# Packing two layers' attention rows from 0 to 79, and giving the weighted scores a third buffer

## The chip, the cores and the metric

One core of a Trainium2 chip runs the whole program. The metric is the device time of one execution in microseconds.

TensorE (PE in the views) multiplies: its stationary operand is loaded first (PEld), then the moving one follows. VectorE (DVE) and ScalarE (ACT) do the work between. The granted clock (PEclk) is the share of TensorE's full clock that the profile recorded; 1.00 is all of it. "Drain" stands here for the time lost when TensorE goes from one size of operand tile to another.

## The reference

Four layers over 2048 rows of 512: a memory-augmented recurrent attention layer (A), a gated feed-forward layer (B), and both again with the same weights.

```python
def _A_ref(x, mem0, Wq, Wk, Wv, Wo, seg_len):      # seg_len 32, 8 memory rows, 32 heads of 128
    ...
    for s in range(n_seg):                          # 64 segments, one after the other
        h = concat([mem, xs])                       # 8 + 32 = 40 rows
        q, k, v = h Wq, h Wk, h Wv
        p = softmax(where(mask, q k^T * scale, -1e9))
        o = (p v) Wo
        mem = o[:8]                                 # the next segment needs it
        outs.append(o[8:])
    ...
x = x + A(layernorm(x)); x = x + B(layernorm(x))
x = x + A(layernorm(x)); x = x + B(layernorm(x))
```

## The kernel before

A step handles segment t of the first attention layer and segment t-6 of the second at once, so there are 70 steps: 6 with layer 0 alone, 58 with both, 6 with layer 1 alone. In each step the 32 heads go through in six groups (five of 6, one of 2). A small planner in the kernel simulates the engines, takes each task with its duration, the buffers it needs and what it depends on, and fixes the order of instructions on every engine. So a change of the buffers or of the task list changes the order everywhere.

The score rows of layer 0 lie in partitions 0 to 39, those of layer 1 in 64 to 103; all stationary operands of scores and transposes are 128x128, padded.

```python
self.qku = [c.tile([P, 3, 2, P], BF16, ...) for i in range(3)]
self.pb  = [c.tile([P, HG, P], BF16, ...) for i in range(2)]        # weighted scores
... # (cut)
plo, phi = (0, LW) if both else ((0, JOFF) if j0 == 0 else (JOFF, LW))   # JOFF 64, LW 104
qc = [(JOFF, 2), (1, L)] if both else [(1, L)]                            # L 40
... # scores
nc.tensor.matmul(s_all(SB)[:, uh - h0 + i, :], lhsT=qku[:, i, 0, :], rhs=fview(qku[:, i, 1, q0:q0 + 1], qc), ...)
... # softmax on VectorE and ScalarE: mask, max, subtract, exp, sum, reciprocal (cut)
# rz: the reciprocal times 1 or 0, by layer
pl.add("DVE", 80, ... out=rz[...], in0=rs[...], in1=self.jm[...], op=ALU.mult ...)
# pb: exp times rz
pl.add("DVE", dve_ns(nj * n), pmul, r=[..., ("rz", gi)], w=[("pb", gi)])
# transposes
nc.tensor.matmul(o_ap, lhsT=pb[:, hl, :], rhs=idn, start=True, stop=True)
```

## Time and profile before

| | before |
|---|---|
| median of the runs beside the changed kernel | 1910.07 us |
| TensorE busy | 94% |
| VectorE busy | 67% |
| start to step 1 (weights arrive) | 106.6 us |
| steps 1 to 5, layer 0 alone | 104.2 us |
| steps 6 to 63, both layers | 1543.5 us |
| step 64 to the end, layer 1 alone and a last feed-forward block | 157.9 us |

The shares and stages are those of one profiled execution (span 1912.2 us). The stages are cut where each step's 128x32 matmuls of line 674 start for the first time; they stand once in every step. I take TensorE as the bound: it is busy for 97% of the two-layer stage, so that a microsecond of its time there should be nearly a microsecond of the whole; in the one-layer stages it has some idle time. The prediction below shows the lines.

### The profile page before, as it was taken

The page shows a single profiled execution, that of the slowest core. Times are in us where ns is not written, and L with a number is a line of the kernel's source. Part 1 is how long each engine was busy: PE and PEld are TensorE (multiplying, and loading weights), DVE is VectorE, ACT ScalarE, POOL GpSimd, SP SyncE. Part 2 cuts the span into 40 slices and gives each one's busy share as a digit, 9 for nine tenths or more (in the row PEclk, how much of TensorE's full clock was granted, in tenths as well). Part 3 has the DMA queues.
Part 4 walks back from the last instruction along what each step waited for, and adds up shares of the span by engine and source line. Part 5 has one row for each costly group of instructions (what it writes and reads, how often), then busy time and mean ns, then how long its engine had stood idle before and what let it go on. Part 6 is the DMA issues. An engine that isn't in the chain of part 4 may idle for free.

```text
span 1912.2 us, 94130 instructions
## 1 busy us (share of the span) xinstructions
PE 1804.7 (94%) x40891; PEld 1565.7 (82%) x41116; DVE 1287.3 (67%) x4238; ACT 1196.6 (63%) x2743; POOL 587.3 (31%) x840
## 2 busy tenths in 40 slices
PE   7988999999999999989999999999999999999986
PEld 3577788988888898878888898889888888988785
DVE  5366576777677666767777777767667666776663
ACT  5655566666666666656666666666666666665553
POOL 6512112332424142332414142332424142323222
PEclk9999999999999999999999999999999999999998
DMA  9723324554636364544635364554646364545543
GB/s 350 252 81 94 97 65 135 150 155 116 187 106 176 108 167 128 144 144 123 180 105 171 108 172 130 144 151 129 180 111 184 81 171 135 145 133 151 146 112 111
DMA packets 130129, 273.83 MB, mean 143 GB/s; under 512 B 29562, under 2 KB 61058, under 8 KB 129714
## 3 DMA queue, kind: packets, MB, share of 16 engines
q0 software_dynamic: 60608, 185.48, 33.8%
q1 hardware_dynamic: 69106, 82.32, 15.2%
q8 instruction: 322, 5.28, 1.2%
q14 instruction: 93, 0.76, 0.1%
HBM read 222.04 MB, written 27.26 MB: 130 GB/s over the span
## 4 chain that ended last, share of the span: by engine, by line
PE 83%; DVE 7%; DMA 3%; ACT 3%; issue 3%; POOL 0%; SPq 0%; DVEq 0%; ACTq 0%; POOLq 0%
PE bank L703 30%; PE bank L802 14%; PE bank L866 10%; PE bank L565 8%; PE bank L674 6%; PE bank L722 4%; PE bank L772 3%; PE bank L785 3%; PE bank L885 3%; DMA vsb<-sst 2%; DVE st L732 1%; ACT otsb L949 1%; PE bank L535 1%; DVE mx L737 1%; DVE pb L758 1%
## 5 line engine op out<-in xcount | busy, mean ns | idle before, releaser
L703 PE MATMUL bank<-hT,wq_sb 128*128 128x80 bf16 (+1 forms) x8960 | 626.1, 198 | 11.1 <-DVE hT L815 5.3
L703 PE MATMUL bank<-hT,wk_sb 128*128 128x80 bf16 (+1 forms) x8960 | 626.2, 199 | 2.9 <-issue 2.9
L949 ACT CAST qku<-bank 128x480 bf16<-128x480 f32 (+3 forms) x770 | 394.6, 513 | 253.1 <-PE bank L703 232.1
L703 PEld LDWEIGHTS <-wq_sb 128*128 128x128 bf16 x8960 | 460.3, 99 | 37.0 <-issue 16.5
L703 PEld LDWEIGHTS <-wk_sb 128*128 128x128 bf16 x8960 | 453.0, 100 | 3.3 <-issue 3.3
L732 DVE TENSOR_TENSOR st<-bank,maskb 64x240 f32<-64x240 f32 (+5 forms) x768 | 284.5, 371 | 223.9 <-PE bank L722 215.8
L802 PE MATMUL bank<-otsb,wo_sb 128*128 128x80 bf16 (+1 forms) x8960 | 372.0, 198 | 12.1 <-ACT otsb L949 9.6
L802 PEld LDWEIGHTS <-wo_sb 128*128 128x128 bf16 x8960 | 340.1, 99 | 24.4 <-issue 15.3
L858 POOL DMA_DIRECT2D wg<-in_B_w_gate_dram x224 | 169.6, 757 | 414.5 <-PE bank L866 382.0
L949 ACT CAST otsb<-bank 128x480 bf16<-128x480 f32 (+3 forms) x420 | 198.9, 486 | 88.8 <-PE bank L785 72.0
L880 POOL DMA_DIRECT2D wd<-in_B_w_down_dram x224 | 159.2, 712 | 280.8 <-PE bank L772 81.7
L523 POOL TENSOR_TENSOR lns<-lns,negh 128x1 f32<-128x1 f32 x78 | 44.2, 568 | 586.6 <-DVE lns L522 281.9
L758 DVE TENSOR_TENSOR pb<-st,rz 104x480 bf16<-104x480 f32 x348 | 206.7, 595 | 7.8 <-PE bank L772 2.7
L744 DVE TENSOR_REDUCE sm<-st 104x6 f32<-104x240 f32 (+5 forms) x420 | 154.0, 367 | 80.0 <-ACT st L742 78.2
L949 ACT CAST ptsb<-bank 128x480 bf16<-128x480 f32 (+3 forms) x343 | 168.6, 496 | 50.0 <-PE bank L772 45.8
L742 ACT ACTIVATE st<-st 104x240 f32<-104x240 f32 (+5 forms) x420 | 161.2, 384 | 57.4 <-DVE st L739 54.9
L866 PE MATMUL bank<-xnT,wg 128*128 128x128 bf16 x1792 | 175.4, 221 | 2.1 <-ACT xnT L949 1.4
L866 PE MATMUL bank<-xnT,wu 128*128 128x128 bf16 x1792 | 174.9, 221 | 2.0 <-DMA wu<-in_B_w_up_dram 2.0
L722 PE MATMUL bank<-qku 128*128 128x80 bf16 (+1 forms) x2240 | 169.3, 198 | 3.7 <-ACT qku L949 1.0
L859 POOL DMA_DIRECT2D wu<-in_B_w_up_dram x224 | 167.7, 749 | 3.0 <-PE bank L866 1.1
L873 DVE SCALAR_TENSOR_TENSOR hff<-th,bank 128x256 bf16<-128x256 f32 x224 | 92.3, 417 | 107.0 <-ACT th L871 104.7
L739 DVE TENSOR_TENSOR st<-st,mx 104x240 f32<-104x240 f32 (+5 forms) x420 | 157.4, 375 | 4.5
(91 smaller groups left out, 2499.3 us busy)
## 6 DMA issues: line engine op xcount, KB each, us to landing
wg<-in_B_w_gate_dram POOLq DMA_DIRECT2D x224, 256.0 KB, 4.4
wu<-in_B_w_up_dram POOLq DMA_DIRECT2D x224, 256.0 KB, 4.8
wd<-in_B_w_down_dram POOLq DMA_DIRECT2D x224, 256.0 KB, 4.8
vsb<-scr SPq DMA_DIRECT2D x512, 48.0 KB
vsb<-sst SPq DMA_DIRECT2D x280, 64.0 KB
scr<-vst SPq DMA_DIRECT2D x128, 96.0 KB
wv_sb<-in_A_Wv_dram SPq DMA_DIRECT2D x4, 1024.0 KB
wq_sb<-in_A_Wq_dram SPq DMA_DIRECT2D x5, 768.0 KB
```

Of the source, the lines that this page charges most:

```text
L703: nc.tensor.matmul(o_ap, lhsT=W[:, c, h * P:(h + 1) * P], rhs=mv(c), start=(c == 0), stop=(c == DC - 1))
L722: nc.tensor.matmul(s_all(SB)[:, uh - h0 + i, :], lhsT=qku[:, i, 0, :], rhs=fview(qku[:, i, 1, q0:q0 + 1], qc), start=True, stop=True)
L732: pl.add("DVE", dve_ns(n, True), lambda gsz=gsz, hs=hs, st=st, SB=SB, pj_=pj_, npj_=npj_, idx=idx: nc.vector.tensor_tensor(out=st[pj_, hs] ...
L739: pl.add("DVE", dve_ns(n), lambda gsz=gsz, hs=hs, st=st, mx=mx: nc.vector.tensor_tensor(out=st[pr, hs], in0=st[pr, hs], in1=mx[pr, hs].uns ...
L742: pl.add("ACT", act_ns(n), lambda hs=hs, st=st: nc.scalar.activation(out=st[pr, hs], in_=st[pr, hs], func=ACTF.Exp, scale=self.scale), r=s ...
L758: nc.vector.tensor_tensor(out=o, in0=st[pr, hs].unsqueeze(1).to_broadcast([npart, 2, gsz, L]), in1=rz[pr, :, 0:gsz].unsqueeze(3).to_broadc ...
L802: nc.tensor.matmul(WB[:, c * ncol:(c + 1) * ncol], lhsT=self.wo[:, h, c * P:(c + 1) * P], rhs=otsb[:, hl, 0:ncol], start=(h == 0 and c == ...
L858: pl.add("POOL", 760, lambda wg=wg, fs=fs: nc.gpsimd.dma_start(out=wg[:], in_=self.wgv[:, :, fs]), r=[("wo", self.H - 1)], w=[("wg", gi)] ...
L859: pl.add("POOL", 760, lambda wu=wu, fs=fs: nc.gpsimd.dma_start(out=wu[:], in_=self.wuv[:, :, fs]), r=[("wo", self.H - 1)], w=[("wu", gi)] ...
L866: nc.tensor.matmul(gu[:, 2 * i + k, :], lhsT=W[:, c, i * P:(i + 1) * P], rhs=xnT[:, c, :], start=(c == 0), stop=(c == DC - 1))
L880: pl.add("POOL", 760, lambda wd=wd, ip=ip: nc.gpsimd.dma_start(out=wd[:], in_=self.wdv[:, 2 * ip:2 * ip + 2, :]), w=[("wd", di)] + (["boot ...
L949: nc.scalar.copy(out=dst, in_=src)
```

## The change

The intent is a denser layout: with both layers in rows 0 to 79 the padded rows and columns go, the copies write contiguous columns, and the room saved in qku pays for a third buffer of weighted scores (pb). In one-layer steps the rows are always 0 to 39 and the product rz, which only separated the layers, goes. A path for transposing by DMA comes with it, but is switched off (DMAT = 0). Cut to its core:

```diff
-LW = JOFF + L                       # 104
+LW = 2 * L                          # 80
-self.qku = [c.tile([P, 3, 2, P], BF16, name=f"qku{i}") for i in range(3)]
+self.qku = [c.tile([P, 3, 2, LW], BF16, name=f"qku{i}") for i in range(3)]
-self.pb = [c.tile([P, HG, P], BF16, name=f"pb{i}") for i in range(2)]
+self.pb = [c.tile([LW, HG, P], BF16, name=f"pb{i}") for i in range(3)]
 ...
+pr = slice(0, ncol)                 # ncol: 80 for both layers, 40 for one
-nc.tensor.matmul(s_all(SB)[:, ...], lhsT=qku[:, i, 0, :], rhs=fview(qku[:, i, 1, q0:q0 + 1], qc), ...)
+nc.tensor.matmul(s_all(SB)[pr, ...], lhsT=qku[:, i, 0, 0:ncol], rhs=qku[:, i, 1, 0:ncol], ...)
 ...
-pl.add("DVE", 80, ... rz ...)
+if both: pl.add("DVE", 80, ... rz ...)
+elif t == self.NSEG and g < 3: pl.add("DVE", 300, ... memset of pb's old columns ...)
 ...
-nc.tensor.matmul(o_ap, lhsT=pb[:, hl, :], rhs=idn, start=True, stop=True)
+nc.tensor.matmul(pt_all(PB)[:, hl, :], lhsT=pb[pr, hl, :], rhs=self.ident[pr, pr], start=True, stop=True)
```

More of the change, by code (lines that the diff above doesn't have):

```diff
@@ L20 @@
 L = MEM + SEG
-JOFF = 64
-LW = JOFF + L
+LW = 2 * L
 KOFF = 8
 XS = 24
+SPT = 1000
+LATT = 2500.0
 SCOL = 24
@@ L368, in __init__ @@
         self.HG = 6
+        self.DMAT = 0
         self.x_in = x_in.rearrange("b s d -> (b s) d")
@@ L397, in setup_tiles @@
         self.maskb = c.tile([P, L], F32, name="maskb")
+        self.mask1 = c.tile([L, L], F32, name="mask1")
         self.jm = c.tile([P, 2], F32, name="jm")
@@ L444, in setup_consts @@
         nc.gpsimd.memset(self.maskb[:], 0.0)
-        tmpm = self.st[0][:, 0, :]
-        nc.gpsimd.memset(tmpm[0:L, :], 0.0)
-        nc.gpsimd.affine_select(out=tmpm[0:L, :], in_=tmpm[0:L, :], pattern=[[-1, L]],
+        nc.gpsimd.memset(self.mask1[:], 0.0)
+        nc.gpsimd.affine_select(out=self.mask1[:], in_=self.mask1[:], pattern=[[-1, L]],
                                 compare_op=ALU.is_ge, fill=NEG, base=0, channel_multiplier=1)
-        nc.gpsimd.memset(tmpm[0:MEM, :], 0.0)
-        nc.sync.dma_start(out=self.maskb[JOFF:LW, :], in_=tmpm[0:L, :])
+        nc.gpsimd.memset(self.mask1[0:MEM, :], 0.0)
+        nc.sync.dma_start(out=self.maskb[L:LW, :], in_=self.mask1[:])
         nc.gpsimd.affine_select(out=self.maskb[0:L, 0:SEG], in_=self.maskb[0:L, 0:SEG], pattern=[[-1, SEG]],
@@ L454, in setup_consts @@
         nc.vector.memset(self.jm[:], 0.0)
-        nc.vector.memset(self.jm[0:JOFF, 0:1], 1.0)
-        nc.vector.memset(self.jm[JOFF:P, 1:2], 1.0)
+        nc.vector.memset(self.jm[0:LW, 1:2], 1.0)
+        nc.vector.memset(self.jm[0:L, 0:1], 1.0)
+        nc.vector.memset(self.jm[0:L, 1:2], 0.0)
         for t_ in self.hT:
@@ L638, in emit_step @@
         ncol = 2 * L if both else L
-        plo, phi = (0, LW) if both else ((0, JOFF) if j0 == 0 else (JOFF, LW))
-        pr = slice(plo, phi)
-        npart = phi - plo
+        pr = slice(0, ncol)
+        npart = ncol
+        nt = -(-ncol // 16) * 16
         hkeys = [("hT", slot, j, k) for j in jobs for k in ("m", "x")]
@@ L653, in pt_all @@
             return B[:, 0:6 * ncol].rearrange("p (h k) -> p h k", h=6)
-        qc = [(JOFF, 2), (1, L)] if both else [(1, L)]
-        q0 = 0 if both else JOFF * j0
         for j in jobs:
@@ L659, in emit_step @@
             b, i = s // BLK, s % BLK
-            row = KOFF if j == 0 else JOFF
+            row = KOFF if j == 0 else KOFF + L + MEM + SEG - XS
             for k in range(4):
@@ L709, in qkcopy @@
                 def qkcopy(nh=nh, pq=pq, qku=qku):
-                    dst = fview(qku[:, 0, 0, q0:q0 + 1], [(P, 2 * nh)] + qc)
-                    src = pq[:, 0:2 * nh * ncol]
-                    if both:
-                        src = src.rearrange("p (m a b) -> p m a b", a=2, b=L)
-                    else:
-                        src = src.rearrange("p (m b) -> p m b", b=L)
-                    return dst, src
+                    return (fview(qku[:, 0, 0, 0:1], [(LW, 2 * nh), (1, ncol)]),
+                            pq[:, 0:2 * nh * ncol].rearrange("p (m b) -> p m b", b=ncol))
                 pl.add("ACT", act_ns(2 * nh * ncol, True), qkcopy, r=[pq], w=[qku])
@@ L721, in sc @@
                     for i in range(nh):
-                        nc.tensor.matmul(s_all(SB)[:, uh - h0 + i, :], lhsT=qku[:, i, 0, :], rhs=fview(qku[:, i, 1, q0:q0 + 1], qc),
+                        nc.tensor.matmul(s_all(SB)[pr, uh - h0 + i, :], lhsT=qku[:, i, 0, 0:ncol], rhs=qku[:, i, 1, 0:ncol],
                                          start=True, stop=True)
@@ L726, in emit_step @@
             gi = self.nxt("st", 2)
-            st, pb, mx, sm, rs = self.st[gi], self.pb[gi], self.mx[gi], self.sm[gi], self.rs[gi]
+            st, mx, sm, rs = self.st[gi], self.mx[gi], self.sm[gi], self.rs[gi]
+            bi = self.nxt("pb", 3)
+            pb = self.pb[bi]
             n = gsz * L
             for idx, j in reversed(list(enumerate(jobs))):
-                pj_ = slice(JOFF if not both and j else 0, JOFF if j == 0 else LW)
-                npj_ = pj_.stop - pj_.start
-                pl.add("DVE", dve_ns(n, True), lambda gsz=gsz, hs=hs, st=st, SB=SB, pj_=pj_, npj_=npj_, idx=idx: nc.vector.tensor_tensor(
+                pj_ = slice(0, L * (idx + 1))
+                npj_ = pj_.stop
+                mk = self.mask1 if j and not both else self.maskb
+                pl.add("DVE", dve_ns(n, True), lambda gsz=gsz, hs=hs, st=st, SB=SB, pj_=pj_, npj_=npj_, mk=mk, idx=idx: nc.vector.tensor_tensor(
                     out=st[pj_, hs], in0=s_all(SB)[pj_, hs, L * idx:L * (idx + 1)],
-                    in1=self.maskb[pj_, :].unsqueeze(1).to_broadcast([npj_, gsz, L]), op=ALU.add),
+                    in1=mk[pj_, :].unsqueeze(1).to_broadcast([npj_, gsz, L]), op=ALU.add),
                     r=[SB] + ([("st", gi, 0)] if both and j == 0 else []), w=[("st", gi, 0), ("st", gi, 1)])
@@ L749, in emit_step, with pmul @@
             kc = KOFF + L * j0
-            pl.add("DVE", 80, lambda gsz=gsz, rs=rs, rz=rz: nc.vector.tensor_tensor(
-                out=rz[pr, 0:nj, 0:gsz], in0=rs[pr, 0:gsz].unsqueeze(1).to_broadcast([npart, nj, gsz]),
-                in1=self.jm[pr, j0:j0 + nj].unsqueeze(2).to_broadcast([npart, nj, gsz]), op=ALU.mult), r=[("rs", gi)], w=[("rz", gi)])
-            def pmul(gsz=gsz, hs=hs, st=st, rz=rz, pb=pb):
+            if both:
+                pl.add("DVE", 80, lambda gsz=gsz, rs=rs, rz=rz: nc.vector.tensor_tensor(
+                    out=rz[pr, :, 0:gsz], in0=rs[pr, 0:gsz].unsqueeze(1).to_broadcast([npart, 2, gsz]),
+                    in1=self.jm[pr, :].unsqueeze(2).to_broadcast([npart, 2, gsz]), op=ALU.mult), r=[("rs", gi)], w=[("rz", gi)])
+            elif t == self.NSEG and g < 3:
+                pl.add("DVE", 300, lambda pb=pb: nc.vector.memset(pb[0:L, :, KOFF:KOFF + L], 0.0), w=[("pb", bi)])
+            def pmul(gsz=gsz, hs=hs, st=st, rs=rs, rz=rz, pb=pb):
                 o = pb[pr, hs, kc:kc + nj * L]
@@ L760, in pmul, with ptr @@
                 else:
-                    nc.vector.tensor_tensor(out=o, in0=st[pr, hs], in1=rz[pr, 0, 0:gsz].unsqueeze(2).to_broadcast([npart, gsz, L]), op=ALU.mult)
-            pl.add("DVE", dve_ns(nj * n), pmul, r=[("st", gi, 0), ("st", gi, 1), ("rz", gi)], w=[("pb", gi)])
-            idn = fview(self.ident[:, q0:q0 + 1], qc)
-            PB = pl.buf(self.bank)
-            def ptr(gsz=gsz, pb=pb, PB=PB):
-                for hl in range(gsz):
-                    o_ap = pt_all(PB)[:, hl, :]
-                    if both:
-                        o_ap = o_ap.rearrange("p (a b) -> p a b", a=2)
-                    nc.tensor.matmul(o_ap, lhsT=pb[:, hl, :], rhs=idn, start=True, stop=True)
-            pl.add("PE", gsz * mm_ns(ncol), ptr, r=[("pb", gi)], w=[PB])
+                    nc.vector.tensor_tensor(out=o, in0=st[pr, hs], in1=rs[pr, 0:gsz].unsqueeze(2).to_broadcast([npart, gsz, L]), op=ALU.mult)
+            pl.add("DVE", dve_ns(nj * n), pmul, r=[("st", gi, 0), ("st", gi, 1), ("rz" if both else "rs", gi)], w=[("pb", bi)])
             pi = self.nxt("ptsb", 3)
             ptsb = self.ptsb[pi]
-            pl.add(("ACT", "DVE"), copy_ns(gsz * ncol), lambda hs=hs, ptsb=ptsb, PB=PB: (ptsb[:, hs, 0:ncol], pt_all(PB)[:, hs, :]), r=[PB], w=[("ptsb", pi)])
+            if g < self.DMAT:
+                pl.add("SP", SPT, lambda hs=hs, ptsb=ptsb, pb=pb: nc.sync.dma_start_transpose(out=ptsb[:, hs, 0:nt], in_=pb[0:nt, hs, :]),
+                       r=[("pb", bi)], w=[("ptsb", pi)], lat=LATT)
+            else:
+                PB = pl.buf(self.bank)
+                def ptr(gsz=gsz, pb=pb, PB=PB):
+                    for hl in range(gsz):
+                        nc.tensor.matmul(pt_all(PB)[:, hl, :], lhsT=pb[pr, hl, :], rhs=self.ident[pr, pr], start=True, stop=True)
+                pl.add("PE", gsz * mm_ns(ncol), ptr, r=[("pb", bi)], w=[PB])
+                pl.add(("ACT", "DVE"), copy_ns(gsz * ncol), lambda hs=hs, ptsb=ptsb, PB=PB: (ptsb[:, hs, 0:ncol], pt_all(PB)[:, hs, :]), r=[PB], w=[("ptsb", pi)])
             if g == 0:
```

## The prediction

> **What bounds the kernel now.** I read the page from the top: busy shares, then the chain that ended last, then the span cut into stages.
>
> ```profile
> PE 1804.7 (94%) x40891; PEld 1565.7 (82%) x41116; DVE 1287.3 (67%) x4238; ACT 1196.6 (63%) x2743; POOL 587.3 (31%) x840
> PE 83%; DVE 7%; DMA 3%; ACT 3%; issue 3%; POOL 0%; SPq 0%; DVEq 0%; ACTq 0%; POOLq 0%
> ```
>
> TensorE is busy 94% of the span and 83% of the final chain is TensorE work; VectorE, which does the softmax, has 67%. A busy TensorE need not be a full one, so I cut the span by the step times (the rare 128x32 matmuls of line 674 mark the 70 steps): weights arrive until about 96 us, steps with only layer 0 run to about 209, steps with both layers to about 1745, steps with only layer 1 to about 1885, then a last feed-forward block. Columns are start:end, length, then busy time and count for PE, PEld, DVE, ACT, POOL, then clock, DMA share, GB/s.
>
> ```profile
> 96.00:209.00 113.00, 98.81 (x2958) 85.95 (x2963) 72.63 (x269) 62.62 (x186) 24.88 (x35) 0.97 0.36 99
> 209.00:1745.00 1536.00, 1485.71 (x33580) 1319.49 (x33764) 1072.78 (x3510) 993.06 (x2215) 455.29 (x633) 1.00 0.49 138
> 1745.00:1885.00 140.00, 126.75 (x3498) 107.83 (x3510) 92.83 (x316) 79.86 (x222) 41.69 (x58) 0.98 0.48 136
> ```
>
> In the two-layer stage PE is busy 1485.7 of 1536 us (97%). In the one-layer stages it is 87% (98.8/113) and 91% (126.8/140): less filler, and the recurrence (a step needs the memory rows that the step before it wrote) shows through. So time is gained or lost almost only by what TensorE does per matmul, or by its waits. How close to its rate it runs is read from start times in the timeline (start, length, then the group):
>
> ```profile
> 900.61 0.31 PE L703 MATMUL bank<-hT,wq_sb 128*128 128x80 bf16 x4
> 900.75 0.31 PE L703 MATMUL bank<-hT,wk_sb 128*128 128x80 bf16 x4
> 900.89 0.31 PE L703 MATMUL bank<-hT,wq_sb 128*128 128x80 bf16 x4
> ...
> 125.46 0.25 PE L703 MATMUL bank<-hT,wq_sb 128*128 128x40 bf16 x4
> 125.56 0.25 PE L703 MATMUL bank<-hT,wk_sb 128*128 128x40 bf16 x4
> 125.74 1.91 PE L674 MATMUL bank<-wv_sb,hT 128*32 128x512 bf16 x32
> 127.59 0.32 PE L722 MATMUL bank<-qku 128*128 128x40 bf16 x6
> ```
>
> Four matmuls of 80 columns start in 0.14 us: about 36 ns each. Four of 40 columns take 0.10 us: 25 ns each. Each has a weight load of 128 columns, so such a load hides inside even 25 ns. The last two lines matter for a rival below: the last of the four at 125.56 began at 125.56 + 3 x 0.025 = 125.635; line 674, which uses the array in 32-column strips, began at 125.74, i.e. 105 ns later where 25 is normal: 80 ns lost going in. Its last matmul (median 379 ns in the view of that line) ends at 127.65, so began at 127.27; the next began at 127.59, 0.32 us later, where four strips of 512 columns side by side need 0.216 (my differences of start times within line 674): about 100 ns lost coming out.
>
> Rows of the table of groups for the parts touched (busy us, mean ns | idle before):
>
> ```profile
> L722 PE MATMUL bank<-qku 128*128 128x80 bf16 x1856 | 143.2, 202 | 2.3 <-ACT qku L949 0.5 <-issue 0.4
> L732 DVE TENSOR_TENSOR st<-bank,maskb 64x240 f32<-64x240 f32 x320 | 126.7, 396 | 34.0 <-PE bank L722 29.7
> L732 DVE TENSOR_TENSOR st<-bank,maskb 104x240 f32<-104x240 f32 x290 | 116.5, 402 | 172.4 <-PE bank L722 169.8
> L750 DVE TENSOR_TENSOR rz<-rs,jm 64x6 f32<-64x6 f32 x30 | 4.5, 151 | 0.2
> L761 DVE TENSOR_TENSOR pb<-st,rz 40x240 bf16<-40x240 f32 x30 | 12.1, 403 | 0.9
> L761 DVE TENSOR_TENSOR pb<-st,rz 64x240 bf16<-64x240 f32 x30 | 11.9, 397 | 0.6
> ```
>
> 40, 64 or 104 partitions cost the same (403, 397; 396, 402): VectorE pays for columns. Waits around the weighted scores, pb:
>
> ```profile
> PEld L772 <- DVE pb L761: 7.4, 14, 2.3
> PEld L772 <- DVE pb L758: 3.6, 11, 0.5
> DVE pb L758 <- PE bank L772: 2.7, 7, 0.9
> ```
>
> **What the Trainium skill says.** (1) "TensorEngine Tiling (Array Packing)", section Key Properties: "Changing tiling mode (not just tile) drains the TensorE". The trace agrees where it can: 80 ns into and 100 ns out of the strip mode of line 674. Its section When to Use Tiling puts a contraction of at most 64 rows, or a stationary side of at most 64 columns, into a half-size tile; no matmul of before with 40 rows or columns shows that. (2) "TensorE: Matmul & The Clock Gate", section Weight-path perf modes: fast weight load is on when the number of weights is 128 and the type is not FP32. A 128-column load hidden within 25 ns agrees; no run here yet shows an 80-column load. (3) The same page, section LDWEIGHTS, gives columns/1.2 ns for a load and says that rows do not count: an estimate from it is 80/1.2 = 67 ns without the fast mode. The trace has the 32-column load of line 674 at 97 ns and the 128-column ones at 99, which speaks for one column per array cycle in the slow mode (estimate for 80 columns: 33 ns, just under the 36 of the matmul). I lean to the second.
>
> **The change, part by part.**
>
> VectorE and ScalarE, two-layer steps: the same instructions with the same columns, on 80 partitions in place of 104 and 40 in place of 64. By the rows above: 0. The copy into qku now writes 80 contiguous columns where it wrote 40+40; before, the split copy took 557 ns and the contiguous copy otsb of the same size 562: 0.
>
> One-layer steps (12 of 70, 6 groups each): the rz product goes, 72 x about 0.155 = 11 us of VectorE, which is not the bound; on the recurrence only the last group counts, so 12 x about 0.15 = 1.8 us at the most. Three clears of pb at the start of the tail cost about 0.3 us each and lie beside other work. Together: -1 us.
>
> Third pb buffer: it can only remove VectorE's wait for the transposes of two groups earlier, 2.7 us in total, and give the order of instructions a little freedom. TensorE's 7.4 + 3.6 us of waits for pb are waits for the product itself, which a buffer does not make earlier. Estimate: -3 us.
>
> Score matmuls, two-layer: 1856 with a stationary side of 128x80 instead of 128x128, and the moving side the same 80 columns, so 36 ns each if the load stays hidden. If the slow load is 33 ns, perhaps 2 ns each are exposed: estimate +4 us. If it is 67 ns, 67 - 36 = 31 each: 1856 x 31 = +58 us. I give the second one chance in five.
>
> Transposes, two-layer: 80 rows, still 128 weight columns: 0.
>
> One-layer steps: scores have a stationary side of 128x40 and transposes one of 40x128. Both are at most 64, so I expect 128x64 and 64x128 tile modes between full-array matmuls, and a drain at every change. In the trace of before I counted unbroken runs of 40-column scores or transposes on TensorE: 101 and 72, of which 153 lie outside the first step, which waits for weights anyhow. Each run pays in and out, about 80 + 100 = 180 ns by the strips: 153 x 0.18 = 27.5 us of TensorE time. In these stages PE is 87 to 91% busy, with idle time mostly at the ends of steps; some drains fall where it would wait anyway. I let 70% reach the end: +19 us.
>
> Sum: -1 - 3 + 4 + 19 = +19 us, i.e. 1929 us.
>
> **The rivals.** (a) The 80-column load is not hidden: +58 in place of +4, so about 1983 us. For it: the skill's formula, and the old layout's padding to 128 columns, which looks deliberate. Against: 97 against 99 ns. (b) Small tiles run inside the full array with no drain: the +19 falls away, and I'd get about 1910 us, unchanged. For it: nothing in the trace shows a 64-wide tile; the strips could be dear because four positions run at once. Against: the skill's words, and equal losses in and out. (c) The freer order pays: with three buffers and shorter one-layer chains the instruction order changes everywhere, and fewer of the 3% gaps of the two-layer stage remain. That stage has 50 us in which PE is not busy; winning a quarter gives -12, so about 1900 us with (b). Against: the listed waits for pb are few us. (d) A new order that is worse by the same amount.
>
> **Range and chances.** The order alone I take as worth 10 us either way. Without (a) the time lies between 1900 and 1945; with (a) between 1950 and 1990. For 8 in 10 I take 1900 to 1965. Faster by 2% means below 1871.6, for which no part of the sum has the size: 0.03. Slower by 2% means above 1948: nearly all of (a)'s 0.2, and a share of drains that cost their full 27 us with a bad order: 0.27. Within 2%: 0.70.
>
> **What would show it.** In the changed trace: starts of successive 80-column scores 36 ns apart (right) or over 60 (a); in one-layer steps a gap of about 100 ns before and after each run of 40-column scores or transposes (right) or 25 (b); the stages 96 to 209 and 1745 to 1885 longer by some 19 us together and the two-layer stage within 10 us of its 1536. What would make me wrong: a two-layer stage longer or shorter by more than 15 us with the same spacing (order), or VectorE instructions with other durations on 80 partitions.

## The result, and the profile after

The changed kernel took 1909.74 us (median of 4 runs, 1909.08 to 1914.27) against 1910.07 (1905.73 to 1910.42). The ratio is 1.0009, 95% interval 0.9987 to 1.003: no difference. Ratios here are the mean time of one kernel's runs over that of the other's of the same rounds, so not quite the ratio of the medians quoted. Where I give an effect in us below, it is the difference of two such ratios times 1910.

The time lies in the stated range, but the step up of 19 us that was forecast is not there. By stages (steps cut as above): columns as in the prediction, before first, then after.

```profile
106.60:210.80 104.20, 91.75 (x2665) 78.83 (x2672) 67.12 (x249) 57.77 (x171) 17.10 (x24) 0.97 0.31 85
210.80:1754.30 1543.50, 1493.21 (x33782) 1326.81 (x33966) 1076.81 (x3524) 997.71 (x2228) 463.03 (x643) 1.00 0.50 139
1754.30:1912.20 157.90, 131.75 (x3400) 109.42 (x3412) 94.05 (x314) 78.85 (x216) 43.32 (x60) 0.94 0.44 124
```

```profile
107.60:216.50 108.90, 104.53 (x2719) 89.59 (x2723) 65.46 (x228) 59.23 (x171) 17.50 (x24) 0.89 0.29 83
216.50:1755.80 1539.30, 1502.66 (x33836) 1335.94 (x34032) 1089.24 (x3569) 990.31 (x2195) 466.09 (x644) 1.00 0.49 139
1755.80:1908.10 152.30, 135.71 (x3343) 110.40 (x3354) 83.88 (x273) 73.77 (x211) 42.95 (x59) 0.98 0.43 124
```

The first one-layer stage is 4.7 us longer than before (104.2) and TensorE is now busy for 96% of it; the two-layer stage is 4 us shorter, the last stage 5.6 us shorter (157.9 before). Together the one-layer stages are 1 us shorter, where 19 longer was foretold. But these lengths are not the change's alone: the granted clock was 0.89 against 0.97 in the first one-layer stage and 0.98 against 0.94 in the last, which goes the same way as the differences. So I read the drains from the gaps between matmuls and from experiments, not from these stages.

The drains first. The timeline of TensorE in a one-layer step (start, length, group):

```profile
127.80 0.25 PE L704 MATMUL bank<-hT,wq_sb 128*128 128x40 bf16 x4
127.89 0.25 PE L704 MATMUL bank<-hT,wk_sb 128*128 128x40 bf16 x4
128.08 0.40 PE L718 MATMUL bank<-qku 128*40 128x40 bf16 x9
128.41 0.27 PE L704 MATMUL bank<-hT,wq_sb 128*128 128x40 bf16 x4
```

The fourth matmul at 127.89 began at 127.89 + 0.075 = 127.965; the scores began at 128.08, about 0.11 us later, where neighbours stand 25 ns apart. From the starts in the trace: the median gap into such a run is 109 ns, out of it 112, and the second score of a run stands 42 ns after the first. So each tile change costs 84 to 87 ns, and a run 84 + 87 + 17 = 188 ns; the prediction had 180. From step 1 on the trace has 277 such changes (a first count, which the next expectation uses, gave 265): at 84 to 87 ns each 23 to 24 us, and with the second matmuls about 26; the prediction had 27.5.

The 80-column loads, in the table of groups:

```profile
L718 PE MATMUL bank<-qku 128*80 128x80 bf16 x1856 | 149.6, 206 | 1.0 <-ACT qku L952 0.3
L718 PEld LDWEIGHTS <-qku 128*80 128x80 bf16 x1856 | 112.7, 121 | 31.5 <-issue 12.7 <-ACT sst L952 5.1 <-ACT st L741 3.0
L750 DVE TENSOR_TENSOR rz<-rs,jm 80x12 f32<-80x12 f32 x290 | 45.7, 158 | 2.0
L763 DVE TENSOR_TENSOR pb<-st,rs 40x240 bf16<-40x240 f32 x60 | 23.6, 394 | 0.4
```

Such a load takes 121 ns where a 128-column one takes 100, and the median gap between scores inside a run is 38 ns instead of 36: a loss of 2 ns as estimated, not 31. VectorE's durations are those of before: 399 ns on 80 partitions against 402 on 104 (mask addition), 394 on 40 against 397 and 403 (weighted scores).

So both costs came as written down. What failed lies on the other side of the sum. That the buffer is used can be seen in the trace: with two buffers a new pb cannot be written before the transposes of two groups earlier have read theirs. I compared these times for the 348 groups of the two-layer steps: in the changed kernel 50 writes begin before the last of those transposes has started, in the kernel before none.

### The profile page after: what moved, and what is told of

Read it like the earlier page. It is cut to its first block, busy times and chain, and to the rows that moved or that the text cites. A ratio compares the mean times of both kernels' runs of the same rounds, so it can differ in the third digit from the quotient of the medians.

```text
span 1908.1 us, 93947 instructions
## 1 busy us (share of the span) xinstructions
PE 1833.2 (96%) x40889; PEld 1586.4 (83%) x41116; DVE 1285.7 (67%) x4213; ACT 1184.2 (62%) x2701; POOL 589.8 (31%) x840
## 4 chain that ended last, share of the span: by engine, by line
PE 84%; DVE 5%; issue 4%; ACT 3%; DMA 3%; POOL 1%; SPq 0%; ACTq 0%; DVEq 0%; POOLq 0%
PE bank L704 29%; PE bank L805 14%; PE bank L869 10%; PE bank L568 8%; PE bank L675 6%; PE bank L718 5%; PE bank L788 4%; PE bank L777 4%; PE bank L888 3%; DVE st L731 1%; DMA vsb<-sst 1%; PE bank L538 1%; DVE pb L760 1%; ACT otsb L952 1%; DMA wu<-in_B_w_up_dram 1%
## 5 line engine op out<-in xcount | busy, mean ns | idle before, releaser
L731 DVE TENSOR_TENSOR st<-bank,maskb 80x240 f32<-80x240 f32 (+1 forms) x732 | 269.8, 369 | 213.2 <-PE bank L718 206.6
L805 PE MATMUL bank<-otsb,wo_sb 128*128 128x80 bf16 (+1 forms) x8960 | 377.5, 199 | 9.2 <-ACT otsb L952 7.3
L805 PEld LDWEIGHTS <-wo_sb 128*128 128x128 bf16 x8960 | 344.2, 100 | 24.3 <-issue 11.5
L760 DVE TENSOR_TENSOR pb<-st,rz 80x480 bf16<-80x480 f32 x348 | 206.6, 594 | 4.8
L741 ACT ACTIVATE st<-st 80x240 f32<-80x240 f32 (+3 forms) x420 | 160.4, 382 | 73.2 <-DVE st L738 71.1
L743 DVE TENSOR_REDUCE sm<-st 80x6 f32<-80x240 f32 (+3 forms) x420 | 152.5, 363 | 72.5 <-ACT st L741 69.3
L952 ACT CAST ptsb<-bank 128x480 bf16<-128x480 f32 (+3 forms) x305 | 150.5, 504 | 44.9 <-PE bank L777 43.1
L718 PE MATMUL bank<-qku 128*80 128x80 bf16 (+1 forms) x2240 | 176.8, 203 | 1.3 <-ACT qku L952 0.3
L718 PEld LDWEIGHTS <-qku 128*80 128x80 bf16 (+1 forms) x2240 | 129.3, 117 | 44.4 <-issue 19.5
L738 DVE TENSOR_TENSOR st<-st,mx 80x240 f32<-80x240 f32 (+3 forms) x420 | 156.2, 372 | 4.3
```

What stands on the lines that cost most here:

```text
L718: nc.tensor.matmul(s_all(SB)[pr, uh - h0 + i, :], lhsT=qku[:, i, 0, 0:ncol], rhs=qku[:, i, 1, 0:ncol], start=True, stop=True)
L731: pl.add("DVE", dve_ns(n, True), lambda gsz=gsz, hs=hs, st=st, SB=SB, pj_=pj_, npj_=npj_, mk=mk, idx=idx: nc.vector.tensor_tensor(out=st[p ...
L738: pl.add("DVE", dve_ns(n), lambda gsz=gsz, hs=hs, st=st, mx=mx: nc.vector.tensor_tensor(out=st[pr, hs], in0=st[pr, hs], in1=mx[pr, hs].uns ...
L741: pl.add("ACT", act_ns(n), lambda hs=hs, st=st: nc.scalar.activation(out=st[pr, hs], in_=st[pr, hs], func=ACTF.Exp, scale=self.scale), r=s ...
L760: nc.vector.tensor_tensor(out=o, in0=st[pr, hs].unsqueeze(1).to_broadcast([npart, 2, gsz, L]), in1=rz[pr, :, 0:gsz].unsqueeze(3).to_broadc ...
L805: nc.tensor.matmul(WB[:, c * ncol:(c + 1) * ncol], lhsT=self.wo[:, h, c * P:(c + 1) * P], rhs=otsb[:, hl, 0:ncol], start=(h == 0 and c == ...
```

## The experiments

Theory A: the drains reach the end, and something else (third buffer, missing rz product, or the luck of the new order) won the same amount. Rival B: the drains fall into waits and cost nothing. If A holds, theory C says that buffer and product have worth of their own, and D that each order of instructions is a draw.

All kernels gave the correct result. The before took 1910.25, 1909.05 and 1911.54 us (11 runs each).

### The drains: full_tile and double_drain

full_tile keeps the order of the changed kernel (nothing that the planner sees changes) and makes the one-layer operands 80 wide:

```diff
-nc.tensor.matmul(s_all(SB)[pr, ...], lhsT=qku[:, i, 0, 0:ncol], ...)
+nc.tensor.matmul(s_all(SB)[0:LW, ...], lhsT=qku[:, i, 0, 0:LW], ...)
-nc.tensor.matmul(pt_all(PB)[:, hl, :], lhsT=pb[pr, hl, :], rhs=self.ident[pr, pr], ...)
+nc.tensor.matmul(pt_all(PB)[:, hl, :], lhsT=pb[0:LW, hl, :], rhs=self.ident[0:LW, pr], ...)
```

> One-layer scores and transposes take 80 stationary columns or rows in place of 40, so the array never leaves its full tile for them; the order of instructions is that of the changed kernel. In the changed kernel's trace 265 tile changes outside the first step cost about 88 ns each, some 23 to 26 us of TensorE time. Theory A (drains reach the end for about 70%, and the new order won as much elsewhere): 1910 - 18 = about 1892 us. Theory B (drains fall where TensorE would have waited for the recurrence): 1910, within 4 us. In both: starts of one-layer scores 25 ns apart from their neighbours in place of 109.

Measured: 1895.43 us (1891.64 to 1896.98), ratio 0.9917 (0.9904 to 0.993). Against the changed kernel's 1.0009 that is 17.6 us. Theory A foretold 18; B has fallen. The gaps are gone, though the expected 25 ns was only half right:

```profile
124.20 0.25 PE L704 MATMUL bank<-hT,wk_sb 128*128 128x40 bf16 x4
124.31 0.50 PE L718 MATMUL bank<-qku 128*80 128x40 bf16 x9
124.65 0.26 PE L704 MATMUL bank<-hT,wq_sb 128*128 128x40 bf16 x4
```

The scores begin 0.11 us after a group of four that itself takes 0.10: no drain. But the nine scores and the step out of them take 0.34 us, 38 ns each: an 80-column load does not hide behind 25 ns. That cost of the slow load, invisible behind 80 moving columns, shows here. Of some 26 us of drains 17.6 reached the end, 68%; the prediction had 70%.

double_drain sets the second head of each run on the full array, so that the tile changes more often:

```diff
+w_ = LW if i == 1 else ncol        # likewise hl == 1 for the transposes
-... [pr, ...], lhsT=qku[:, i, 0, 0:ncol]
+... [0:w_, ...], lhsT=qku[:, i, 0, 0:w_]
```

> In one-layer steps the second head of each run is done on the full array, so most runs change the tile four times in place of two: about 20 us more of TensorE time in the one-layer steps, same order. Theory A (drains reach the end for 70%): +14 to +18 us, about 1926. Theory B (drains fall into waits): under +5 us.

Measured: 1958.11 us (1953.88 to 1960.84), ratio 1.0245 (1.0227 to 1.0262), 45 us above the changed kernel. The direction is A's, the size a miss. Part of it is my count: from step 1 on the trace has 599 tile changes, not 277. Those with a gap under 0.2 us (571 and 246, so that waits are left out) take 59.6 us above 25 ns each instead of 22.1, so 37 more, not 20. The rest shows in the stages:

```profile
111.60:236.10 124.50, 121.16 (x2727) 100.44 (x2727) 66.02 (x228) 59.94 (x170) 17.52 (x24) 0.88 0.25 71
236.10:1781.40 1545.30, 1519.16 (x34026) 1340.74 (x34024) 1089.74 (x3569) 990.83 (x2196) 466.18 (x644) 1.00 0.49 139
1781.40:1959.00 177.60, 165.06 (x3355) 131.00 (x3355) 84.62 (x273) 74.70 (x211) 42.99 (x59) 0.88 0.37 106
```

TensorE is busy 97% and 93% of the one-layer stages, so no slack is left to take the drains, and the granted clock is 0.88 in both (full_tile: 0.97 and 0.93; the changed kernel, with drains too: 0.89 and 0.98). Over the whole execution it was 0.978 to 0.983 in the four runs, against 0.990 to 0.993 in the changed kernel. By the estimate under "How much is luck" some 10 of the 45 us go with the clock. That drains lower the clock is not shown: the changed kernel has them in both stages and a low clock in one.

### The slow load: wide_scores

```diff
+m_ = P if both else ncol
-... [pr, ...], lhsT=qku[:, i, 0, 0:ncol]
+... [0:m_, ...], lhsT=fview(qku[:, i, 0, 0:1], [(1, m_)])   # runs on into the neighbouring columns
```

> Two-layer scores again with 128 stationary columns (the 48 extra ones are neighbouring data, their rows of the result are not read); order as in the changed kernel. The changed trace has 38 ns between scores where before had 36. Theory A (80-column load costs about 2.5 ns in two of three of the 1856 scores): -3 us, about 1907. Rival (the load's longer time, 121 ns against 100, also holds up the instructions after it): -10 us or more. If neither: 0.

Measured: 1908.2 us (1904.1 to 1914.39), ratio 0.999 (0.9972 to 1.0008), 3.6 us below the changed kernel, with overlapping intervals. The trace shows the mechanism plainly: loads back to 100 ns, gaps back to 36.

```profile
L719 PE MATMUL bank<-qku 128*128 128x80 bf16 x1856 | 144.2, 202 | 0.3 <-ACT qku L953 0.3
L719 PEld LDWEIGHTS <-qku 128*128 128x128 bf16 x1856 | 98.9, 100 | 32.4 <-issue 12.7 <-ACT sst L953 5.1 <-ACT st L742 3.0
```

The large rival is out; -3 fits, but the times alone do not tell it from 0. The stages help: the two-layer stage took 1535.0 us against 1539.3 in the changed kernel, in the same order and at a clock of 1.00 in both.

### The third buffer: two_pb and before_pb3

```diff
-self.pb = [... for i in range(3)]        # two_pb, from the changed kernel
+self.pb = [... for i in range(2)]
-bi = self.nxt("pb", 3)
+bi = self.nxt("pb", 2)
-elif t == self.NSEG and g < 3:
+elif t == self.NSEG and g < 2:
```

> The changed kernel with two pb buffers; the planner's order changes with it. Theory A (the third buffer is what won back the cost of the drains): +15 to +20 us, about 1927. Theory B (the third buffer removes only 2.7 us of VectorE waits, the rest is chance of the order): 1910 within 8 us, either way.

Measured: 1921.91 us (1920.24 to 1925.57), ratio 1.0059 (1.0046 to 1.0072): 9.6 us above the changed kernel, between the two theories. So I put the third buffer alone into the kernel before. It did not fit there (with the padded qku the program does not build), hence tighter heads, with stationary operands that still read 128 columns and run on into the next head:

```diff
-self.qku = [c.tile([P, 3, 2, P], ...)]
+self.qku = [c.tile([P, 3, 2, LW], ...)]              # LW 104
-self.pb = [c.tile([P, HG, P], ...) for i in range(2)]
+self.pb = [c.tile([P, HG * 96 + 32], ...) for i in range(3)]
-lhsT=qku[:, i, 0, :]
+lhsT=fview(qku[:, i, 0, 0:1], [(1, P)])
-lhsT=pb[:, hl, :]
+lhsT=pb[:, hl * 96:hl * 96 + P]
 ... (and the index bi of the changed kernel)
```

> The kernel before with a third pb buffer and nothing else of the change (the heads of pb and qku are packed closer to make room; operands still 128 wide, rows still 0 to 39 and 64 to 103). Theory C (a third buffer lets the planner find a better order, worth the 11.5 us that two_pb lost): about 1898 us. Theory D (each new order is a draw, and the buffer has no worth of its own beyond its 2.7 us of waits): anywhere within 10 us of 1910, either side.

Measured: 1900.33 us (1897.0 to 1905.1), ratio 0.9956 (0.9941 to 0.9972): -8.4 us. The same size in both layouts, in the direction of C. Its trace has 55 early writes of the kind counted above. The wait that I had taken for the buffer's worth was as small with two buffers in the changed layout as it is in the kernel before; the view of waits of two_pb:

```profile
DVE pb L760 <- PE bank L777: 2.9, 7, 0.9
```

What the buffer removed stands elsewhere, among TensorE's waits in the two-layer stage: at its 512-column products of line 565 (568 after) and its transposes of line 535 (538), both waiting for ScalarE. Two lines each of before and two_pb, with two buffers, then the first of these waits in before_pb3 and full_tile, with three:

```profile
PE bank L565 <- ACT otsb L949: 8.7, 12, 0.7
PE bank L535 <- ACT xn L526: 4.4, 6, 1.6
PE bank L568 <- ACT xvl L952: 6.6, 14, 0.5
PE bank L538 <- ACT xn L529: 4.7, 7, 1.6
PE bank L565 <- ACT xvl L951: 0.3, 1, 0.3
PE bank L568 <- ACT xvl L952: 0.3, 1, 0.3
```

The first wait is 6.6 us in the two kernels with two buffers whose traces hold every matmul of that line (two_pb, before_norz), and 8.7 in the other three, where some records are missing; in all nine with three buffers it is at most 0.5. The second is over 4 us in four of the five (0.4 in before_order31) and at most 0.2 in the nine. Between two_pb and the changed kernel the two make some 10 us, and the two-layer stage is 10.2 us shorter (1549.5 against 1539.3). That this is the whole worth of the buffer is an inference from the sizes: in before_pb3 a wait for a DMA grew meanwhile (vsb<-sst, 3.6 to 11.5 us).

### The missing product: before_norz and full_tile_rz

```diff
+if both:                                  # before_norz, from the kernel before
     pl.add("DVE", 80, ... rz ...)
-in1=rz[pr, 0, 0:gsz]
+in1=rs[pr, 0:gsz]
```

> The kernel before without the rz product in one-layer steps. full_tile's last stage is 11 us shorter than that of before, and two_pb's by 6 although it pays for drains. Theory C (the shorter chain of VectorE work in one-layer steps): last stage 5 to 10 us shorter, about 1903 us. Theory D (the order): within 8 us of 1910, and the last stage not consistently shorter.

Measured: 1903.79 us (1900.68 to 1904.16), ratio 0.9965 (0.9952 to 0.9978): -6.7 us. The total is what C expected, but the last stage (154.2 us against 157.9) shrank less than its 5 to 10; the first one-layer stage is 102.2 against 104.2.

```diff
+else:                                     # full_tile_rz, from full_tile
+    pl.add("DVE", 80, ... out=rz[pr, 0:1, 0:gsz], in0=rs[...], in1=self.jm[pr, 0:1] ...)
-in1=rs[pr, 0:gsz]
+in1=rz[pr, 0, 0:gsz]
```

> full_tile with the rz product put back in one-layer steps. Theory C: about 1902, the last stage 5 to 10 us longer than full_tile's 146.6. Theory D: within 8 us of 1895, either way.

Measured: 1903.6 us (1896.32 to 1906.16), ratio 0.9959 (0.994 to 0.9979): 8 us above full_tile, in the size of C, though the last stage (148.8 against 146.6) grew less than C asked, and the first one-layer stage by 4.7 (105.9 against 101.2, at a clock of 0.94 against 0.97). The six executions differ more than those of other kernels: two took 1896.3 and 1896.4 us at a mean clock of 0.993, as long as full_tile's, and three 1905.3 to 1906.2 at 0.988 to 0.990.

```profile
L754 DVE TENSOR_TENSOR rz<-rs,jm 40x6 f32<-40x6 f32 x60 | 9.0, 150 | 0.5
L754 DVE TENSOR_TENSOR rz<-rs,jm 40x2 f32<-40x2 f32 x12 | 1.8, 153 | 0.4
```

These are all the instructions put back: 10.8 us of VectorE time. Whether most of that came back as time of the program, as 8 us would say, hangs on the clock; see the end of the next part.

### How much is luck of the order: four kernels

One constant of the planner's model changes, and with it the order; work and buffers do not.

```diff
-TO_PE = 32.0
+TO_PE = 31.0          # before_order31, full_tile_order31; 33.0 in the other two
```

> The kernel before, with one constant of the planner's model (a latency of 32) set to 31: the same work and buffers, another order of instructions. Theory C (buffer and product have worth of their own): 1910 within 4 us. Theory D (every order is a draw): a difference of 5 to 12 us, either side.

Measured: 1905.74 us, ratio 0.9977 (0.9957 to 0.9997).

> As before_order31 with the constant at 33. Theory C: within 4 us of 1910. Theory D: 5 to 12 us, either side.

Measured: 1914.4 us, ratio 1.0017 (0.9997 to 1.0037).

> full_tile with that constant at 31. Theory C: 1895 within 4 us, so below both orders of before by more than 10. Theory D: a difference from 1895 of 5 to 12 us, and the two groups overlap.

Measured: 1887.91 us, ratio 0.9881 (0.9862 to 0.99).

> As full_tile_order31 with the constant at 33. Theory C: 1895 within 4 us. Theory D: 5 to 12 us, either side.

Measured: 1892.28 us, ratio 0.9912 (0.9889 to 0.9934).

So an order is worth some 4 us either way: three orders of before spread over 8 us (0.9977, 1, 1.0017), three of full_tile over 7 (0.9881, 0.9912, 0.9917). The groups stay 11 us apart at the nearest, and their means differ by 18. D alone cannot make that gap. Nor does C's "within 4" hold everywhere: full_tile_order31 lies 7 us below full_tile. One pair of kernels cannot show an effect of 7 to 10 us against such a spread; that buffer and product each came out with the same sign and size in two layouts is what speaks for the split, and it is less firm than their sum.

I had left one rival untested, the granted clock. In every kernel with five runs or more the executions with the lower mean clock tend to be the longer ones (correlations of -0.5 to -0.97). A straight line through the 104 executions whose clock is on record, with a mean of its own for each kernel (and for each before), gives 1.1 us more for every 0.001 of clock less. An estimate at equal clock, if this line also holds between kernels: drains 13 us; third buffer 11 and 12; rz 7 and 4; the orders of before within 6 us and those of full_tile within 5, the nearest two 7 apart, the means 13. The buffer then stands well clear of the orders. The product does not: before_norz is only 2 us below before_order31.

### Both repairs: all_full

The changed kernel with full-array operands in one-layer steps and 128 stationary columns in all scores; same order.

```diff
-... [pr, ...], lhsT=qku[:, i, 0, 0:ncol]
+... [0:P, ...], lhsT=fview(qku[:, i, 0, 0:1], [(1, P)])
-lhsT=pb[pr, hl, :], rhs=self.ident[pr, pr]
+lhsT=pb[0:LW, hl, :], rhs=self.ident[0:LW, pr]
```

> The changed kernel with both repairs: no 64-wide tiles, and 128 stationary columns for all scores; same order. If the gains add up: full_tile's 1895 less 2 (wide_scores), less 384 one-layer scores at 38 ns where 25 is possible (up to 5 us of TensorE time, some of it in waits) = 1888 to 1893 us, faster than both kernels by about 1%. Rival (the gains overlap): 1895.

Measured: 1889.84 us (1889.1 to 1891.42), ratio 0.9897 (0.9884 to 0.9911): 1% faster than both kernels. It is 3.8 us below full_tile by the ratios, as if the gains added, but the two intervals just overlap. The two-layer stage (1534.9 us against 1540.8 in full_tile, same order) repeats what wide_scores showed.

## Why the prediction was wrong

| term of its sum | predicted | measured |
|---|---|---|
| drains of the half tiles, one-layer steps | +19 | +17.6 (changed kernel against full_tile) |
| 80-column loads, two-layer steps | +4 | +3.6, not resolved in the totals (against wide_scores) |
| rz product gone, pb clears | -1 | -6.7 and -8, not clear of order and clock (before_norz; full_tile_rz) |
| third pb buffer | -3 | -9.6 and -8.4 (two_pb; before_pb3) |
| sum | +19 | about +5 from the parts; +1.7 by the ratio, interval -2.5 to +5.7 |

- **The costs were right,** in mechanism and in size: 188 ns per run against 180, 68% reaching the end against 70% (about half, by the estimate at equal clock), 2 ns per slow load, though the load itself is nearer 38 ns than the estimated 33. Rival (a), a load of 67 ns, is out: with only 40 moving columns to hide it, an 80-column load let scores start every 38 ns. Rival (b), no drains, is out.
- **The step that failed is the term "Third pb buffer".** It read "it can only remove VectorE's wait for the transposes of two groups earlier, 2.7 us in total". It removed 8 to 10 us in both layouts. A wait in the trace counts what is left after the order was made: here only 2.7 us stood at the buffer. The early writes (none before, 50 after) show the new freedom in use. What went with it were TensorE's waits for ScalarE at other work, the 512-column products and the transposes of line 535 or 538: some 11 us with the two buffers of two_pb and before_norz, at most 0.7 with three. Why the planner's order put them there is not shown.
- **The second mis-sized term is the rz product.** "On the recurrence only the last group counts, so 12 x about 0.15 = 1.8 us at the most": the pairs of kernels gave 6.7 and 8 of its 11 us. If that holds, more than the last group's chain lies on the path of a one-layer step. But an order alone moved the time by 4 us, and the clock took half of the second difference in the estimate above, so this step stays open.
- **Rival (c), "the freer order pays",** had the right idea and the right order of size (-12) and was set aside because "the listed waits for pb are few us". That is the argument that failed.
- **Chances:** within 2% had 0.70 and came true, as did the range, but by cancelling: about 21 us of costs met about 16 of gains, of which 4 had been foreseen.

## What to carry to other kernels

Where a planner or a person has ordered the work around a scarce buffer, the waits on that buffer can say little of its worth, as here: try one more and measure. Cutting padding off a stationary operand can cost time: here loads of 80 columns took 121 ns where those of 128 took 100, and with 40 rows or columns each excursion from the full array cost 0.19 us. Before a difference of some us is explained, compare the granted clocks. When a change that mixes costs and gains comes out at zero, undo the costs one by one with the order held fixed; here that turned 0% into 1%.

## What the Trainium skill lacked or had wrong

- "TensorEngine Tiling (Array Packing)", Key Properties, says that a change of tiling mode drains the engine, without a figure. The runs show 84 to 87 ns for each change and 17 ns more at the second score. It doesn't say either that ordinary matmuls with a side of 40 pay it without anyone asking for tiles; here they did (gaps of 109 ns where full-size operands have 25).
- "TensorE: Matmul & The Clock Gate", LDWEIGHTS, gives columns/1.2, an estimate of 67 ns for 80 columns. The runs show a score every 38 ns with 80-column loads and 40 moving columns. Nor do the loads' own times follow the columns: 98 ns with 40, 121 with 80, 100 with 128. That fast loading asks for 128 columns (Weight-path perf modes) agrees: 25 ns apart and 100 ns long with 128, 38 and 121 with 80; but inside a run 40-column loads too let scores start 25 ns apart.
- "Perfetto Trace Analysis", Optimization Strategy, says that consistent bubbles can mean too little room for the next tile. The reverse needs a warning: a shortage worth 8 to 10 us showed only 2.7 us of waits on the buffer, and some 11 us of waits at two other places.
